# A third raw weight buffer and a token-by-token end of each second product, in a fused retention, routing and MLP kernel

## The chip, the cores and the metric

The kernel runs on one core of a Trainium2 chip. The metric is the device time of one execution in microseconds (us). TensorE (PE, with its weight loads as PEld) does the matrix products, VectorE (DVE), ScalarE (ACT) and GpSimd (POOL) the elementwise work, and SyncE (SP) issues most of the transfers. Each engine runs its own instructions strictly in their order and waits on semaphores for the others.

## The reference

```
x = retention(q, k, v)              # 8 x 8 heads, 576 positions, to 4608 tokens x 512
logits = x @ w_gate                 # 8 experts, each takes exactly 576 tokens, greedily by logit
for e in range(8):
    out[mask_e] = relu(x[mask_e] @ w1[e]) @ w2[e]        # 512 -> 1024 -> 512
h = relu(out @ w_in)                # 512 -> 2048
return (h * h) @ w_out              # 2048 -> 512
```

All data are float32 and all large products have float32 accuracy: each operand is split into a rounded high part and the rest (the low part), and a product is made of three: high weights by high data, low weights by high data, high weights by low data (PAIRS).

## The kernel before, in words

**Attention** (0 to about 165 us of the profiled execution) makes x in transposed tiles X, and converts the second MLP's weights into a DRAM tensor wd beside it. The table `rt` of 510 columns, which the router needs, comes in one transfer among the first loads (line 108), and `Router.start` makes constants from its later columns after the fourth token tile. Then the router places the tokens of the first expert, and x goes to DRAM token by token (xd).

**The main part** (218 to 1514 us) goes expert by expert. `moe(k)` works on the 576 tokens of expert k in two parts of 288. Each part has eight steps f: a first product into a PSUM tile `mm` (line 802, 12 matmuls of 288 columns), the relu and split of its result into the tile `h` (ACT L807, DVE L808), and the second product of the step two before (LAG = 2) into four accumulators `acc` (L785, 12 matmuls). After the last second product of a part the accumulators are copied to YH by ACT (L791) and their rest to YL by DVE (L792). There are four `acc` buffers, so the first second product of part 1 waits until YL has been taken of part 0. That place is called the part border below.

After each expert one or two blocks `mlp(j)` of 384 tokens follow, twelve in all (j = 0 to 11: one after experts 0, 2, 4, 6, two after 1, 3, 5, 7). A block has 16 steps: first product (L865, 12 matmuls of 384 columns), then ACT L871 (relu), DVE L873 (square), ACT L875 (high part of h), DVE L842 (low part of h, called `low`), and the second product two steps late (L849, 9 matmuls: three token tiles by three pairs). At the end of a block two second products are left, those of f = 14 and f = 15. They run one after the other, and after f = 15 ACT copies each token tile's accumulator to `ot` (L853), which POOL scatters to the output (L828).

**The weight stream.** Weights come in chunks of 128 x 1024 float32, 16 per expert and 7 per block (nine of the 16 MLP chunks stay on chip, tile `big`). `pump()` is called once per step. It splits one chunk, if one has been fetched and the weight tiles have room: ACT writes the high parts of w1 and w2 (L628, two instructions), POOL the low part of w1 (L629), DVE the low part of w2 (L630). Then it fetches one chunk into a buffer `raw` (SP, L639), if fewer than two are fetched and not split. There are two `raw` buffers, so the transfer of chunk i waits until ACT, POOL and DVE are done with chunk i - 2.

```
if i < st["fetched"] and i < st["used"] + 3 and not fetch_only:
    raw = raws.pop(i)
...
    nc.gpsimd.tensor_sub(w1[:, 1], raw[:, :512], w1[:, 0].bitcast(F32))
    nc.vector.tensor_sub(w2[:, 1], raw[:, 512:], w2[:, 0].bitcast(F32))
...
if i < len(stream) and i < st["split"] + 2:
```

**The router** for expert k + 1 runs in small pieces (`slot`) between the products of expert k and the following blocks: comparisons on DVE (L398, L427, L432), small matmuls on PE into `rps` (L421, L431, L480). It is done for experts 0 to 7 before expert 6's products, so experts 6 and 7 run without it. Tokens of the next expert are gathered from xd (POOL) and turned on PE (L716).

The order of every engine's instructions is that of the program; there is no scheduler.

Of the kernel before, what the change touches and what calls it, by code (L numbers as in the profile page):

```python
# [6 lines left out]
F32 = mybir.dt.float32  # L7
R = mybir.dt.float32r
# [61 lines left out]
def attention(tc, a, X, idn, rt, filler):  # L70

    nc = tc.nc
    L = rt.L
    with ExitStack() as c:
# [30 lines left out]
        wg = cn.tile([128, 4, 32], F32, name="wg")  # L105
        nc.vector.memset(wg, 0.0)
        nc.sync.dma_start(wg[:, :, :NE], a["wg"])
        nc.sync.dma_start(rt.f, a["rt"])
        load(3, 0, 2)
        load(2, 2, 3)  # L110
        load(4, 0, 2)
# [111 lines left out]
        for t in range(NT):  # L223
            if t + 2 < NT:
                turn_k(t + 2)
            if t + 1 < NT:
                weigh(t + 1)
                scores(t + 1)
            if t + 5 < NT:
                load(t + 5, 0, 2)  # L230
            if t + 3 < NT:
                load(t + 3, 2, 3)
            if t + 2 < 9:
                decay(t + 2)
            before(t)
            if t >= 4 and t % 2 == 0:
                next(todo, None)
            values(t)
            if t % 9 != 8:
                state(t)  # L240
            if t == NT - 2:
                ready = rt.prep(0, 32)
            if t >= NT - 2:
                next(ready)
            if t == 3:
                rt.start()
            next(filler, None)
        last = [gate(32, 35), gate(35, 36, "sp")]
        for g in last:
# [7 lines left out]
def route_tables():  # L257
    i = np.arange(128)
    tri = (i[:, None] < i[None, :]).astype(np.float32)
    u = np.zeros((128, 72), np.float32)  # L260
    j = np.arange(72)
    u[:72] = j[:, None] < j[None, :]
    thr = np.zeros((4, 16), np.float32)
    off = 0
    for r, step in enumerate(STEPS):
        thr[r] = np.arange(16) * step - off
        off += step
    sel = np.zeros((128, 4, 8), np.float32)
    for tl in range(4):
        sel[tl * 8:tl * 8 + 8, tl] = np.eye(8)  # L270
    f = np.concatenate([np.tile(thr.reshape(1, 64), (128, 1)),
                        np.tile(8.0 - np.arange(8), (128, 1)),
                        np.tile(128.0 * np.arange(36), (128, 1)),
                        i[:, None].astype(np.float32),
                        np.zeros((128, 8)),
                        np.tile(np.arange(8.0), (128, 1)),
                        np.tile(i, (128, 1)),
                        tri, u,
                        i[:, None] // 16 == np.arange(8),
                        i[:, None] % 16 == np.arange(16),  # L280
                        np.where(i < 8, CAP, BIG)[:, None],
                        sel.reshape(128, 32),
                        ], axis=1)
    return np.ascontiguousarray(f, np.float32)


# [6 lines left out]
class Router:  # L293
# [6 lines left out]
    def __init__(self, tc, pool):  # L300
        self.nc, self.ps = tc.nc, None
        t = pool.tile
        self.L = t([128, NT, 8], F32, name="L")
        f = self.f = t([128, 510], F32, name="rt")
        self.thr = f[:, 0:64].rearrange("p (r j) -> p r j", r=4)
        self.w8 = f[:, 64:72]
        self.t128 = f[:, 72:108]
        self.pcol = f[:, 108:109]
        self.e8 = f[:, 117:125]
        self.m8, self.m16 = f[:, 453:461], f[:, 461:477]  # L310
        self.c8 = f[:, 477:478]
        self.io = t([128, 128, 12], FH, name="io")
        self.b = t([128, 128 + 72], FH, name="rtb")
        self.tri, self.u = self.b[:, 0:128], self.b[:, 128:200]
        self.OH = [t([128, 128, 12], FH, name=f"OH{i}") for i in range(2)]
        self.sel = self.OH[0].rearrange("p s t -> p (s t)")[:, :512].rearrange("p (t m) -> p t m", t=4)
        self.ones = t([128, 128], FH, name="ones")
        self.U = t([128, NT], F32, name="U")
        self.AS = t([128, NT], F32, name="AS")
        self.C = t([128, 8], F32, name="C")  # L320
        self.idx = t([128, NT], I32, name="idx")
        self.es = t([1, NE], I32, name="es")
        self.A = t([128, NT + 12, 8], FH, name="A")
        self.V = t([128, NT, 8], F32, name="V")
        self.m = t([128, NT], F32, name="m")
        self.vm = t([128, NT], F32, name="vm")
        self.vu = t([128, NT], F32, name="vu")
        self.ki = t([128, 4, NT], I32, name="ki")
        self.kf = t([128, 2, NT], F32, name="kf")
        self.k2 = t([128, NT], F32, name="k2")  # L330
        self.B = t([128, 2], F32, name="B")
        self.G = t([128, NT + 4, 16], FH, name="G")
        self.c4 = t([128, 64], FH, name="c4")
        self.S8 = t([128, 16], FH, name="S8")
        self.dg = t([128, 8, 8], F32, name="dg")
        self.cc = t([128, 8], F32, name="cc")
        self.cx = t([128, 16, 8], FH, name="cx")
        self.cf = t([128, 16, 8], F32, name="cf")
        self.jm = t([128, 16], F32, name="jm")
        self.jk = t([128, 16], F32, name="jk")  # L340
        self.GT = t([128, 2, NT], F32, name="GT")
        self.NEW = t([128, 2, NT, 8], FH, name="NEW")
        self.wn = t([128, 16], FH, name="wn")
        self.nn = t([128, 48], F32, name="nn")
        self.DT = t([128, 2, NT], FH, name="DT")
        self.tot = t([72, 128], FH, name="tot")
        self.sl = t([128, 4, NT], F32, name="sl")
        self.si = t([128, 3, NT], I32, name="si")
        self.sb = t([128, 2, NT], FH, name="sb")
        self.h5 = t([128, NT, 5], FH, name="h5")  # L350
        self.HC = t([128, NT, 10], FH, name="HC")
        self.ids = t([128, 10], F32, name="ids")

    def start(self):
        v, f = self.nc.vector, self.f
        for x, c in ((self.sel, 0.0), (self.ones, 1.0), (self.U, 1.0), (self.AS, 0.0), (self.C, float(CAP)),
                     (self.A, 0.0), (self.G, 0.0)):
            v.memset(x, c)
        v.tensor_copy(self.io, f[:, 125:253].unsqueeze(2).to_broadcast([128, 128, 12]))
        v.tensor_copy(self.b, f[:, 253:453])  # L360
        v.tensor_copy(self.sel[:, :, 0:8], f[:, 478:510].rearrange("p (t e) -> p t e", t=4))

    def p(self):
        return self.ps.tile([128, 128], F32, name="rps")
# [220 lines left out]
def body(tc, a, out):  # L585
    nc = tc.nc
    with ExitStack() as ctx:
# [8 lines left out]
        rt = Router(tc, gp)  # L596
# [23 lines left out]
        def pump(fetch_only=False):  # L620

            i = st["split"]
            if i < st["fetched"] and i < st["used"] + 3 and not fetch_only:
                raw = raws.pop(i)
                w1 = wk.tile([128, 2, 512], R, name="w1", bufs=3)
                w2 = wk.tile([128, 2, 512], R, name="w2", bufs=5)
                for w, c in ((w1, raw[:, :512]), (w2, raw[:, 512:])):
                    nc.scalar.activation(w[:, 0], c, AF.Copy)  # L628
                nc.gpsimd.tensor_sub(w1[:, 1], raw[:, :512], w1[:, 0].bitcast(F32))  # L629
                nc.vector.tensor_sub(w2[:, 1], raw[:, 512:], w2[:, 0].bitcast(F32))  # L630
                chunks[i] = (w1, w2)
                st["split"] += 1
            i = st["fetched"]
            if i < len(stream) and i < st["split"] + 2:
                kind, k, f = stream[i]
                if kind == "e" and k not in ev:
                    return
                raw = raws[i] = wk.tile([128, 1024], F32, name="raw", bufs=2)
                nc.sync.dma_start(raw, wd[f] if kind == "m"  # L639
                                  else a["we"][bass.ds(ev[k], 1), f].rearrange("o p c -> (o p) c"))  # L640
                st["fetched"] += 1
# [135 lines left out]
        def moe(k):  # L777
# [16 lines left out]
            for part in range(2):  # L794
                turned(5 * k + (5 if part else 3))
                for f in range(8):
# [6 lines left out]
                                             X[xi][:, g, 288 * part:288 * part + 288],  # L803
                                             start=(g == 0 and i == 0), stop=(g == 3 and i == 2))
                    slot(True)
                    h = wk.tile([128, 2, 384], R, name="h", bufs=4)
                    nc.scalar.activation(h[:, 0, :288], p[:, :288], AF.Relu)  # L807
                    nc.vector.scalar_tensor_tensor(h[:, 1, :288], p[:, :288], 0.0, h[:, 0, :288].bitcast(F32),  # L808
                                                   op0=OP.max, op1=OP.subtract)
# [24 lines left out]
        def mlp(j):  # L834
# [6 lines left out]
                    s, h = lows.pop()  # L841
                    nc.vector.tensor_sub(h[:, 1], s, h[:, 0].bitcast(F32))  # L842

            def mm2(f, w2, h):
                if f == 0:
                    acc.extend(ps.tile([128, 512], F32, name="acc", bufs=4) for _ in range(3))
                for t in range(3):
                    for i, (wi, xi) in enumerate(PAIRS):
                        nc.tensor.matmul(acc[t], h[:, xi, t * 128:(t + 1) * 128], w2[:, wi],  # L849
                                         start=(f == 0 and i == 0), stop=(f == 15 and i == 2))  # L850
# [5 lines left out]
            for f in range(16):  # L856
# [14 lines left out]
                nc.scalar.activation(r, p[:, :384], AF.Relu)  # L871
                s = r
                nc.vector.tensor_mul(s, p[:, :384], r)  # L873
                h = wk.tile([128, 2, 384], R, name="h", bufs=4)
                nc.scalar.activation(h[:, 0], s, AF.Copy)  # L875
                lows.append((s, h))
                q.append((f, w2, h))
# [3 lines left out]
                low()  # L881
                if f >= LAG:
                    slot()
            while q:
                mm2(*q.pop(0))

        turner, keeper, parter = turn_back(), stay(), part()
        while 0 not in listed:
# [38 lines left out]
```

## Time and profile before

| | us |
|---|---|
| median of 3 runs | 1531.27 (1529.21 to 1531.87) |
| the profiled execution | 1525.86 |
| its span, first to last instruction | 1524.1 |
| PE busy in it | 1462.2 (96%) |
| DVE busy | 963.5 (63%) |
| ACT busy | 675.0 (44%) |
| POOL busy | 468.5 (31%) |

The span is what the trace shows; the execution's own time has 1.8 us around it. A busy PE is not a PE at its peak, since matmuls overlap: what counts below is the time in which PE waits, and for whom. The mean granted TensorE clock of the execution was 0.992.

### The profile page before, as it was taken

The numbers are of one execution on the slowest core, as the hardware profiler recorded it, in microseconds if no ns is written. First come the engines' busy times: TensorE is split into PE (matmuls) and PEld (weight loads), VectorE is DVE, ScalarE is ACT, GpSimd is POOL, SyncE is SP. The second block draws the span as 40 slices with busy tenths as digits, with TensorE's granted clock in tenths as the row PEclk, the third lists the DMA queues.
The fourth block names the chain that finished last, engine by engine and source line by source line (L and its number), as shares of the span: only waits on it lengthen the run. The fifth ranks groups of instructions, "written<-read, shape, count | busy, mean of one in ns | idle before, by whom it ended". The sixth has DMA issues, their size and how long they took to land.

```text
span 1524.1 us, 27399 instructions
## 1 busy us (share of the span) xinstructions
PE 1462.2 (96%) x10599; PEld 1324.4 (87%) x10599; DVE 963.5 (63%) x1965; ACT 675.0 (44%) x1349; POOL 468.5 (31%) x410
## 2 busy tenths in 40 slices
PE   7998879999999999999999999999999999999997
PEld 6777768888988898889988899899888999999896
DVE  5999768766765657557765667567646455454341
ACT  6766644444433434334433344344334344444332
POOL 4454134544312224124213143233122431242110
PEclk9999979999999999999999999999999999999999
DMA  9999567224511224225313143234112351252110
GB/s 337 347 365 352 197 203 257 97 70 133 158 56 72 87 93 154 70 97 157 107 56 96 58 148 127 68 123 161 56 61 89 123 174 64 64 180 95 57 49 21
DMA packets 64210, 201.14 MB, mean 132 GB/s; under 512 B 8400, under 2 KB 8656, under 8 KB 64080
## 3 DMA queue, kind: packets, MB, share of 16 engines
q1 hardware_dynamic: 58128, 179.99, 35.2%
q0 software_dynamic: 5952, 19.40, 3.6%
q8 instruction: 83, 1.36, 0.4%
q14 instruction: 47, 0.39, 0.1%
HBM read 172.10 MB, written 27.26 MB: 131 GB/s over the span
## 4 chain that ended last, share of the span: by engine, by line
PE 73%; DVE 11%; DMA 6%; issue 5%; ACT 4%; POOL 0%; SPq 0%; ACTq 0%; DVEq 0%; POOLq 0%
PE mm L865 24%; PE acc L849 23%; PE acc L785 9%; PE mm L802 8%; DMA raw<-we 4%; DVE w L630 3%; PE px L205 2%; ACT w L628 1%; PE sc L165 1%; PE mm L716 1%; PE rps L508 1%; DVE cb L569 1%; DVE G L398 1%; DVE A L169 1%; DMA raw<-wd 1%
## 5 line engine op out<-in xcount | busy, mean ns | idle before, releaser
L629 POOL TENSOR_TENSOR w<-raw,w 128x512 fp32r<-128x512 f32 x212 | 278.0, 1311 | 825.8 <-ACT w L628 729.0
L630 DVE TENSOR_TENSOR w<-raw,w 128x512 fp32r<-128x512 f32 x212 | 265.4, 1252 | 228.7 <-ACT w L628 224.4
L628 ACT ACTIVATE w<-raw 128x512 fp32r<-128x512 f32 x424 | 243.3, 621 | 205.7 <-DMA raw<-we 163.0
L849 PE MATMUL acc<-big,h 128*128 128x512 f32 x972 | 246.0, 397 | 0.0
L785 PE MATMUL acc<-h,w 128*128 128x288 f32 x1536 | 224.4, 296 | 12.0 <-DVE YL L792 9.7
L785 PEld LDWEIGHTS acc<-h,w 128*128 128x128 f32 x1536 | 208.4, 188 | 14.6 <-DVE YL L792 11.6
L849 PEld LDWEIGHTS acc<-big,h 128*128 128x128 f32 x972 | 180.1, 188 | 35.4 <-DVE h L842 0.3
L871 ACT ACTIVATE r<-mm 128x384 f32<-128x384 f32 x192 | 93.9, 489 | 237.7 <-PE mm L865 217.2
L875 ACT ACTIVATE h<-r 128x384 fp32r<-128x384 f32 x192 | 100.9, 525 | 216.8 <-DVE r L873 216.8
L849 PE MATMUL acc<-w,h 128*128 128x512 f32 x756 | 190.9, 396 | 2.9 <-DVE h L842 2.9
L873 DVE TENSOR_TENSOR r<-mm,r 128x384 f32<-128x384 f32 x192 | 105.9, 551 | 125.5 <-ACT r L871 125.3
L865 PE MATMUL mm<-YH,big 128*128 128x384 f32 x864 | 173.4, 342 | 0.0
L849 PEld LDWEIGHTS acc<-w,h 128*128 128x128 f32 x756 | 139.3, 188 | 29.6 <-DVE h L842 3.7
L802 PE MATMUL mm<-XH,w 128*128 128x288 f32 x1024 | 161.0, 300 | 0.8 <-ACT XH L724 0.7
L865 PEld LDWEIGHTS mm<-YH,big 128*128 128x128 f32 x864 | 152.1, 188 | 7.7 <-ACT YH L791 0.9
L842 DVE TENSOR_TENSOR h<-r,h 128x384 fp32r<-128x384 f32 x192 | 110.9, 577 | 65.7 <-ACT h L875 65.7
L802 PEld LDWEIGHTS mm<-XH,w 128*128 128x128 f32 x1024 | 143.8, 190 | 2.0 <-ACT XH L724 1.1
L865 PE MATMUL mm<-YH,w 128*128 128x384 f32 x672 | 133.3, 339 | 0.0
L865 PEld LDWEIGHTS mm<-YH,w 128*128 128x128 f32 x672 | 117.6, 188 | 4.3
L865 PE MATMUL mm<-YL,big 128*128 128x384 f32 x432 | 93.4, 338 | 0.0
L802 PE MATMUL mm<-XL,w 128*128 128x288 f32 x512 | 89.0, 295 | 0.0
L865 PEld LDWEIGHTS mm<-YL,big 128*128 128x128 f32 x432 | 77.3, 188 | 0.3 <-DVE YL L792 0.2
(171 smaller groups left out, 1713.5 us busy)
## 6 DMA issues: line engine op xcount, KB each, us to landing
raw<-we SPq DMA_DIRECT2D x128, 512.0 KB, 3.6
raw<-wd SPq DMA_DIRECT2D x84, 512.0 KB, 3.2
qk<-att SPq DMA_DIRECT2D x36, 512.0 KB, 7.0
craw<-wm SPq DMA_DIRECT2D x32, 512.0 KB, 6.7
v<-att SPq DMA_DIRECT2D x36, 256.0 KB, 5.4
wd<-cb SPq DMA_DIRECT2D x32, 256.0 KB, 5.4
xd<-YH SPq DMA_DIRECT2D x18, 256.0 KB, 3.5
xd<-YL SPq DMA_DIRECT2D x18, 256.0 KB, 3.6
```

The lines of the kernel that those rows point to most:

```text
L205: nc.tensor.matmul(px[o:o + 64, g, :], V[t][:, g, lo:lo + 64], D[t]["A"][i][:, g, :], start=(ph == 0), stop=True)
L628: nc.scalar.activation(w[:, 0], c, AF.Copy)
L629: nc.gpsimd.tensor_sub(w1[:, 1], raw[:, :512], w1[:, 0].bitcast(F32))
L630: nc.vector.tensor_sub(w2[:, 1], raw[:, 512:], w2[:, 0].bitcast(F32))
L785: nc.tensor.matmul(acc[part][d][:, :288], w2[:, wi, d * 128:(d + 1) * 128], h[:, xi, :288], start=(f == 0 and i == 0), stop=(f == 7 and i ...
L802: nc.tensor.matmul(p[:, :288], w1[:, wi, g * 128:(g + 1) * 128], X[xi][:, g, 288 * part:288 * part + 288], start=(g == 0 and i == 0), stop ...
L842: nc.vector.tensor_sub(h[:, 1], s, h[:, 0].bitcast(F32))
L849: nc.tensor.matmul(acc[t], h[:, xi, t * 128:(t + 1) * 128], w2[:, wi], start=(f == 0 and i == 0), stop=(f == 15 and i == 2))
L865: nc.tensor.matmul(p[:, :384], w1[:, wi, g * 128:(g + 1) * 128], Y[xi][:, g, o:o + 384], start=(g == 0 and i == 0), stop=(g == 3 and i == 2))
L871: nc.scalar.activation(r, p[:, :384], AF.Relu)
L873: nc.vector.tensor_mul(s, p[:, :384], r)
L875: nc.scalar.activation(h[:, 0], s, AF.Copy)
```

## The change

A third `raw` buffer is made and `pump` fetches up to three chunks that are not split. Its room comes from two places: `h` has three buffers in place of four, and the router's table is taken in two transfers, of which the larger (`rf`, 360 columns) lies in the attention's pool and is given up with it. In `mlp` the last two second products are taken token tile by token tile: f = 14 and 15 for tile 0, then for tile 1, then for tile 2.

```
-        nc.sync.dma_start(rt.f, a["rt"])
+        nc.sync.dma_start(rt.f, a["rt"][:, :150])
+        rf = cn.tile([128, 360], F32, name="rf")
+        nc.sync.dma_start(rf, a["rt"][:, 150:])
...
-                rt.start()
+                rt.start(rf)
...
-            if i < len(stream) and i < st["split"] + 2:
+            if i < len(stream) and i < st["split"] + 3:
...
-                raw = raws[i] = wk.tile([128, 1024], F32, name="raw", bufs=2)
+                raw = raws[i] = wk.tile([128, 1024], F32, name="raw", bufs=3)
...
-                    h = wk.tile([128, 2, 384], R, name="h", bufs=4)
+                    h = wk.tile([128, 2, 384], R, name="h", bufs=3)
...
-            def mm2(f, w2, h):
+            def mm2(f, w2, h, tiles=range(3)):
...
-                for t in range(3):
+                for t in tiles:
...
-                h = wk.tile([128, 2, 384], R, name="h", bufs=4)
+                h = wk.tile([128, 2, 384], R, name="h", bufs=3)
...
-            while q:
-                mm2(*q.pop(0))
+            for t in range(3):
+                for x in q:
+                    mm2(*x, tiles=(t,))
```

The orders of DVE, ACT and POOL do not change: every instruction stands where it stood. Two orders change. On PE, at the end of each block, here the fourth (j = 3, after expert 2), whose last two second products read a streamed weight tile `w` (f = 14) and a kept one `big` (f = 15). Before:

```order
L421 MATMUL rps<-A,G 128x64
L849 MATMUL acc<-w_7786,h 128x512 x9
L849 MATMUL acc<-big,h 128x512 x9
L802 MATMUL mm<-XH,w_7862 128x288 x8
L802 MATMUL mm<-XL,w_7862 128x288 x4
L716 MATMUL mm<-idn,xg 128x128 x4
```

and in the changed kernel (its line numbers are 3 higher here):

```order
L424 MATMUL rps<-A,G 128x64
L852 MATMUL acc<-w_7790,h 128x512 x3
L852 MATMUL acc<-big,h 128x512 x3
L852 MATMUL acc<-w_7790,h 128x512 x3
L852 MATMUL acc<-big,h 128x512 x3
L852 MATMUL acc<-w_7790,h 128x512 x3
L852 MATMUL acc<-big,h 128x512 x3
L805 MATMUL mm<-XH,w_7866 128x288 x8
L805 MATMUL mm<-XL,w_7866 128x288 x4
L719 MATMUL mm<-idn,xg 128x128 x4
```

The first matmul that reads the last h (f = 15) moves from the tenth place of these 18 to the fourth, and the last matmul of tile 0 from the twelfth to the sixth, that of tile 1 from the fifteenth to the twelfth.

On SP, each fetch stands one fetch earlier against everything else in the queue. Here the end of expert 1 and the two blocks behind it, where `raw<-we` is an expert's chunk, `raw<-wd` an MLP chunk, and the load of `es` reads the router's choice of expert. Before:

```order
L639 ISA
L639 DMA raw<-we 128x1024
L639 DMA raw<-wd 128x1024 x9
L697 TENSOR_LOAD es
L697 ISA x2
L639 DMA raw<-wd 128x1024 x5
L639 ISA
L639 DMA raw<-we 128x1024
```

and in the changed kernel:

```order
L642 ISA
L642 DMA raw<-we 128x1024
L642 DMA raw<-wd 128x1024 x10
L700 TENSOR_LOAD es
L700 ISA x2
L642 DMA raw<-wd 128x1024 x4
```

Ten MLP chunks stand ahead of the load of `es` where nine stood, and no fetch has moved behind a wait that it did not stand behind.

## Rows read from the trace of the kernel before

**Rows 1.** The page: its head and PE's row, busy us and share.

```profile
span 1524.1 us, 27399 instructions
...
PE 1462.2 (96%) x10599; PEld 1324.4 (87%) x10599; DVE 963.5 (63%) x1965; ACT 675.0 (44%) x1349; POOL 468.5 (31%) x410
```

**Rows 2.** PE's waits: who waited for whom, us in total, times, longest us.

```profile
PE acc L785 <- DVE YL L792: 9.7, 8, 1.7
...
PE rps L431 <- DVE cx L427: 2.9, 6, 1.1
...
PE acc L785 <- DVE h L808: 2.3, 2, 1.5
```

**Rows 3.** Waits of all engines, same columns.

```profile
DVE w L630 <- ACT w L628: 224.4, 156, 3.2
...
ACT w L628 <- DMA raw<-we: 163.0, 88, 6.0
...
ACT w L628 <- DMA raw<-wd: 39.6, 22, 3.1
```

**Rows 4.** Chain that ended last, expert 6 from 1223 us: start, us, what.

```profile
1223.47 3.56 DMA raw<-we
...
1228.30 1.38 DVE w L630
...
1229.78 3.32 DMA raw<-we
...
1238.36 1.59 PE mm L802 x12
```

**Rows 5.** Timeline, expert 6's part border: start, us, engine line [idle before, releaser].

```profile
1233.19 1.15 ACT L628 ACTIVATE w<-raw 128x512 fp32r<-128x512 f32 x2 [1.84 <-DMA raw<-we]
...
1234.37 1.36 DVE L630 TENSOR_TENSOR w<-raw,w 128x512 fp32r<-128x512 f32 x1 [1.56 <-ACT w L628]
...
1236.03 1.53 DVE L792 TENSOR_TENSOR YL<-acc,YH 128x288 fp32r<-128x288 f32 x4
...
1236.52 1.84 PE L785 MATMUL acc<-h,w 128*128 128x288 f32 x12 [1.30 <-DVE YL L792]
```

**Rows 6.** Timeline, expert 0's part border.

```profile
252.46 1.46 DVE L630 TENSOR_TENSOR w<-raw,w 128x512 fp32r<-128x512 f32 x1 [0.24 <-ACT w L628]
...
258.00 1.85 PE L785 MATMUL acc<-h,w 128*128 128x288 f32 x12 [1.72 <-DVE YL L792]
```

**Rows 7.** Timeline, expert 1's part border, whose wait is the shortest.

```profile
391.71 1.06 PE L785 MATMUL acc<-h,w 128*128 128x288 f32 x6 [0.58 <-DVE YL L792]
```

**Rows 8.** Durations of two DVE groups: count, ns least/median/most, first and last start.

```profile
L630 DVE TENSOR_TENSOR w<-raw,w x212: 672/1365/2487, 205.4 to 1481.1; 128x512 fp32r<-128x512 f32 x106
...
L427 DVE TENSOR_TENSOR cx<-cc,rt x48: 291/292/1367, 230.6 to 1090.9; 128x128 f16<-128x128 f32 x48
```

**Rows 9.** Timeline, end of block j = 3: second product f = 14, then h of f = 15.

```profile
679.18 2.31 PE L849 MATMUL acc<-w,h 128*128 128x512 f32 x9
...
679.86 0.52 ACT L875 ACTIVATE h<-r 128x384 fp32r<-128x384 f32 x1 [1.75 <-DVE r L873]
680.41 0.56 DVE L842 TENSOR_TENSOR h<-r,h 128x384 fp32r<-128x384 f32 x1 [0.59 <-ACT h L875]
...
681.33 2.26 PE L849 MATMUL acc<-big,h 128*128 128x512 f32 x9
```

**Rows 10.** Timeline, end of block j = 0, the same instructions.

```profile
355.79 0.52 ACT L875 ACTIVATE h<-r 128x384 fp32r<-128x384 f32 x1 [2.09 <-DVE r L873]
356.35 0.56 DVE L842 TENSOR_TENSOR h<-r,h 128x384 fp32r<-128x384 f32 x1 [0.59 <-ACT h L875]
...
356.48 2.37 PE L849 MATMUL acc<-big,h 128*128 128x512 f32 x9
```

**Rows 11.** Timeline, end of block j = 2, the same instructions.

```profile
550.47 2.30 PE L849 MATMUL acc<-w,h 128*128 128x512 f32 x9
550.48 0.53 ACT L875 ACTIVATE h<-r 128x384 fp32r<-128x384 f32 x1 [1.51 <-DVE r L873]
```

**Rows 12.** Timeline, the end of the last block and the tail of the kernel.

```profile
1508.90 0.53 ACT L875 ACTIVATE h<-r 128x384 fp32r<-128x384 f32 x1 [0.62 <-DVE r L873]
...
1509.63 2.23 PE L849 MATMUL acc<-w,h 128*128 128x512 f32 x9
...
1512.59 2.00 ACT L853 ACTIVATE ot<-acc 128x512 f32<-128x512 f32 x3 [3.16 <-PE acc L849]
1513.46 0.99 POOL L828 DMA_INDIRECT out<-ot,idx  x1 [31.48 <-ACT ot L853]
...
1516.03 0.97 POOL L828 DMA_INDIRECT out<-ot,idx  x1 [0.22 <-issue]
```

**Rows 13.** Timeline, the first microseconds: the router's table, the next load, PE.

```profile
7.64 0.34 SPq L108 DMA_DIRECT2D rt<-rt  x1
...
8.02 0.43 SPq L85 DMA_DIRECT2D qk<-att  x1
...
15.56 0.66 PE L143 MATMUL pr<-idn,qk 128*128 128x128 f32 x4
```

More of the change, by code (lines that the diff above doesn't have):

```diff
@@ L283, in route_tables @@
                         ], axis=1)
+    f = np.concatenate([f[:, :125], f[:, 453:478], f[:, 125:453], f[:, 478:]], axis=1)
     return np.ascontiguousarray(f, np.float32)
@@ L303, in __init__ @@
         self.L = t([128, NT, 8], F32, name="L")
-        f = self.f = t([128, 510], F32, name="rt")
+        f = self.f = t([128, 150], F32, name="rt")
         self.thr = f[:, 0:64].rearrange("p (r j) -> p r j", r=4)
@@ L309, in __init__ @@
         self.e8 = f[:, 117:125]
-        self.m8, self.m16 = f[:, 453:461], f[:, 461:477]
-        self.c8 = f[:, 477:478]
+        self.m8, self.m16 = f[:, 125:133], f[:, 133:149]
+        self.c8 = f[:, 149:150]
         self.io = t([128, 128, 12], FH, name="io")
@@ L352, in __init__, with start @@
         self.ids = t([128, 10], F32, name="ids")
-    def start(self):
-        v, f = self.nc.vector, self.f
+    def start(self, f):
+        v = self.nc.vector
         for x, c in ((self.sel, 0.0), (self.ones, 1.0), (self.U, 1.0), (self.AS, 0.0), (self.C, float(CAP)),
@@ L358, in start @@
             v.memset(x, c)
-        v.tensor_copy(self.io, f[:, 125:253].unsqueeze(2).to_broadcast([128, 128, 12]))
-        v.tensor_copy(self.b, f[:, 253:453])
-        v.tensor_copy(self.sel[:, :, 0:8], f[:, 478:510].rearrange("p (t e) -> p t e", t=4))
+        v.tensor_copy(self.io, f[:, 0:128].unsqueeze(2).to_broadcast([128, 128, 12]))
+        v.tensor_copy(self.b, f[:, 128:328])
+        v.tensor_copy(self.sel[:, :, 0:8], f[:, 328:360].rearrange("p (t e) -> p t e", t=4))
     def p(self):
```

## Prediction

> **What bounds the kernel now.** I read the page first. PE is busy for 1462.2 of 1524.1 us [rows 1], so no change of transfers can give more than the 62 us between them, and only where PE itself waits. The waits of PE come next. The largest is at the part border: the first second product of part 1 waits for YL, eight times, once per expert, 9.7 us in all [rows 2]. Behind it, and also within the experts' stages, stand waits for DVE's router work (L431 for cx, 2.9 us) and for h (2.3 us) [rows 2]. No row has PE waiting for a weight tile.
>
> Weights still matter, one step removed. In the waits of all engines ACT's split waits 163.0 us for expert chunks and 39.6 us for MLP chunks, and DVE's part of the split waits 224.4 us for ACT [rows 3]. Both engines are in order, so whatever stands behind the split waits too. The chain of waits of expert 6, which runs without a router, shows what sets that pace: transfer 3.56 us, ACT, DVE 1.38 us, and the next transfer into the same buffer, 6.31 us from 1223.47 to 1229.78 [rows 4]. With two buffers that is 3.16 us a chunk. PE needs 1.59 us for the 12 matmuls of a first product [rows 4] and as much for those of a second, 3.18 us a step. The loop and PE are tied, and the loop never gets ahead.
>
> At the part border this lateness reaches PE. In expert 6 ACT's split starts at 1233.19 after 1.84 us of waiting for the chunk, DVE's part after 1.56 us for ACT, YL comes at 1236.03, and PE has waited 1.30 us when it starts at 1236.52 [rows 5].
>
> **The third raw buffer.** Nothing is added on ACT, POOL or DVE: their orders are the same, word for word. What changes is when a chunk lands. With three buffers the loop of 6.31 us [rows 4] carries three chunks, 2.1 us each, against 3.2 us of PE per step; a chunk then lies ready about 3 us before its split, and ACT splits it as soon as it comes to it. In expert 6 the split at 1233.19 would start 1.84 us earlier, DVE's part at least 1.56 us earlier, and 1.56 is more than the 1.30 that PE waited: the wait goes.
>
> What the eight borders give has two ends. The lower: DVE can move forward by at least its own wait before L630, and that is least in expert 0, 0.24 us against a PE wait of 1.72 [rows 6]; in the other seven I grant no more than the shortest PE wait of all, 0.58 in expert 1 [rows 7]. That is 0.24 + 7 x 0.58 = 4.3 us. The upper is all of 9.7. I take 8.0: seven of the eight look like expert 6, and in expert 0 much of DVE's time at the border is router work that stays.
>
> The two other waits of rows 2, 2.9 + 2.3 = 5.2 us, lie between 0 and 5.2. They end with DVE work that stands behind a late L630 but is itself long; I take 1.5, nearer to nothing, since there DVE is mostly busy and not waiting.
>
> In the MLP blocks a chunk is needed only every second or third step, and ACT's wait there is a fraction of the 39.6 us, none of it in front of PE: nothing.
>
> **The token-by-token end.** Here is a cost. Before, the first matmul on h of f = 15 had all nine of f = 14 in front of it; now three. Take block j = 3 [rows 9]. Nine matmuls last from 679.18 to 681.33, 0.24 us each. After three PE is at 679.90. The high part of h is done at 679.86 + 0.52 = 680.38. From the end of that instruction to PE's start I take 0.17 us, as in block 0 where the high part ends at 356.31 and PE starts at 356.48 [rows 10]. So PE waits until 680.55, 0.65 us; after two matmuls it is at 681.03, and the low part (680.97 + 0.17 = 681.14) costs 0.11 more. 0.76 us, and block 6 shows the same pattern: 1.5 us together. In block 0 PE had already waited for this h, and the six matmuls of f = 14 that filled the time until 356.48 now come after it: PE does two matmuls on the high part, waits to 357.08 for the low part, and has 13 left where it had 9 - the end moves from 356.48 + 9 x 0.24 = 358.64 to 357.08 + 13 x 0.24 = 360.20, 1.5 us. In blocks 2 and 5 the high part is ready at 551.01 + 0.17 for a PE at 550.47 + 0.71 [rows 11], just in time, and the low part costs 0.1 each. In the other seven it is early; in the last one the high part is done at 1509.43 and wanted at 1510.3 [rows 12]. The sum is 1.5 + 1.5 + 0.2 = 3.2 us. Bounds: 2 us, if the earlier chunks also relieve ACT and DVE in block 0; 5.6, if blocks 1, 4 and 7 fall to the state of block 3 (3 x 0.8 more).
>
> **The tail.** In the last block tile 0 is finished six matmuls earlier, tile 1 three. Today ACT copies three tiles from 1512.59, 0.67 us each, and POOL scatters them from 1513.46, one each 1.29 us, the last at 1516.03 [rows 12]. With tile 0 earlier by 6 x 0.23 = 1.4 us the first two scatters are over by 1514.5, and the third waits only for its own copy: last matmul as before, copy until 1514.65, scatter at 1514.85. That is 1.2 us off the end. It cannot be more, since the third tile ends as before, and nothing if POOL's queue has another delay.
>
> **Edits at no cost.** Three h buffers: h of step f takes the buffer of f - 3, whose second product stands ahead of the first product of f on PE, and ACT waits for that one anyway. The second transfer of the table costs SP another 0.34 us behind 7.64 and moves the load at 8.02 [rows 13]; PE first reads that load at 15.56, 7.5 us later. If the cover failed it would be about 0.4 us, once.
>
> **A rule that speaks against it.** DVE's L630 takes 0.672 us at best and 1.365 in the median, and cx (L427) 0.292 in the median and 1.367 at worst [rows 8]: something holds DVE for about the length of another engine's instruction. The Trainium skill, page "SBUF — State Buffer", section "SBUF: two separate sides", says that DVE with two SBUF inputs and GpSimd lock one shared pair of ports, whole instruction by whole instruction. By that rule a POOL split that runs earlier leaves L630 and hits router work in its stead; the trace agrees that such hits exist (cx 1.367), and no run here shows how many there would be. It is the slower rival below, and is not in the sum.
>
> **The sum.** -8.0 (borders) - 1.5 (other waits) + 3.2 (block ends) - 1.2 (tail) = -7.5 us. The profiled execution, 1525.86 with its span of 1524.1, would be 1518.4 with a span of 1516.6. It lies 5.4 us under the median of the three timed runs, so I take the difference to the median: 1531.27 - 7.5 = 1523.8 us. With all gains at their best and the block ends at 2: 9.7 + 5.2 + 1.2 - 2 = 14.1 less, 1517.2. With all at their worst: 4.3 less and 5.6 more, 1532.6.
>
> **The rivals.** About 0.2% (3.1 us) is what a measurement of this kernel can tell from no change.
> - DVE, not the chunk, holds the border. For it: the routers run in experts 0 to 5, and in expert 0 the wait for the chunk was only 0.24 of 1.72 us [rows 6]. Against it: expert 6 without a router waits 1.30 [rows 5]. Gains then are 3.0 at the borders and 1.2 at the tail, the cost 3.2: 1531.27 - 1.0 = 1530.3 us. Chance 0.17.
> - The third buffer does not make chunks early, because the transfers themselves are slower with one more under way. For it: a transfer in the loop takes 3.3 to 3.6 us already [rows 4]. Against it: three chunks in 6.3 us leave a third of the time over. Only the block ends and the tail remain: +3.2 - 1.2 = 1533.3 us. Chance 0.08.
> - Slower: POOL's earlier splits hit DVE's router work in experts 0 to 5. One hit is 1.367 - 0.292 = 1.1 us [rows 8]. It costs only where PE waits for that piece. Ten more such hits, among the 96 chunks of these six experts, eat the 7.5 us and 3.1 beyond; with ten to twelve it would be about 1535 us. Against it: L630 itself gets shorter by up to 0.69 us where the hit leaves it. Chance 0.07.
>
> **How the numbers follow.** The forecast has 0.68. Nearly all of it is faster by over 0.2% (below 1528.2); with a little of the first rival faster is 0.68, the same 0.24 (most of the first two rivals), slower 0.08. The range of the forecast alone is 1518 to 1529; to hold 8 in 10 it goes on to the first rival, 1518 to 1530.5, and leaves out the other two and what lies below.
>
> **What would show it.** Right: ACT's wait for raw falls from 202.6 us to under 40; PE's wait for YL from 9.7 to under 3; a new wait of PE L852 for ACT h or DVE h at the ends of blocks 0, 3 and 6, 2 to 4 us in all; the last scatter 1.2 us nearer to the last matmul. Wrong: YL's wait still near 9 us with chunks early (first rival), ACT's wait for raw still over 100 us (second), cx or L398 longer on average and PE's waits for `rps` grown by 8 us or more (third). What would make the number wrong with the mechanism right is the share of the 5.2 us of router waits that goes, and block ends that are later than here.

## The result and the profile after

The changed kernel takes 1511.61 us (median of four runs, 1509.73 to 1512.18), the kernel before 1530.4 beside it (1529.21 to 1531.87). The ratio is 0.9883 with a 95% interval of 0.9858 to 0.9908: faster by 1.2%, 18.8 us. The prediction was 1523.8 us, 7.5 us faster, with 1518.0 as the lower end of its range. The direction was right, the size less than half.

The profiled execution after took 1512.18 us, 13.7 us less than that of before. The page's head, PE's row and DVE's part of the split (these answer to [rows 1] and [rows 8]):

```profile
span 1510.4 us, 27450 instructions
...
PE 1461.7 (97%) x10599; PEld 1325.1 (88%) x10599; DVE 933.6 (62%) x1965; ACT 688.6 (46%) x1349; POOL 468.6 (31%) x410
...
L633 DVE TENSOR_TENSOR w<-raw,w 128x512 fp32r<-128x512 f32 x212 | 226.9, 1070 | 193.5 <-ACT w L631 192.5
```

PE's work is the same to 0.5 us; what went is its idle time. DVE is busy 30 us less although it runs the same instructions in the same order.

PE's waits after, in the columns of [rows 2]:

```profile
PE acc L852 <- DVE h L845: 2.9, 2, 1.5
...
PE acc L852 <- ACT h L878: 1.8, 3, 1.1
...
PE rps L434 <- DVE cx L430: 0.7, 2, 0.5
```

The largest row of before, PE for YL (9.7 us), is gone from the list altogether, as is the wait for DVE's h in the experts (2.3). The wait for cx fell from 2.9 to 0.7. The three waits for ACT's h at the ends of blocks, 1.8 us, are new: they are the price of the new order. DVE's h above them stood there before with the same 2.9, and is not of the new order.

The waits of the other engines, in the columns of [rows 3]:

```profile
DVE w L633 <- ACT w L631: 192.5, 140, 1.6
...
ACT w L631 <- PE acc L788: 62.1, 93, 1.4
...
ACT w L631 <- DMA raw<-we: 15.8, 17, 2.6
```

ACT's wait for an expert chunk fell from 163.0 to 15.8 us. In its place stands a wait for PE's second products, 62.1 us: the chunk now lies ready so early that the split waits for a weight tile to come free. DVE still waits 192.5 us for ACT, but by at most 1.6 us at a time where it was 3.2, and no row of PE waiting for YL is left.

Expert 6's chain of waits shows it at a glance, beside [rows 4]. It was a loop of transfer and split; now PE is all of it, row after row:

```profile
1220.85 1.58 PE acc L788 x12
1222.43 1.60 PE mm L805 x12
1224.03 1.58 PE acc L788 x12
1225.61 1.60 PE mm L805 x12
1227.21 1.58 PE acc L788 x12
```

At its part border the timeline, beside [rows 5], reads:

```profile
1222.46 0.63 ACT L631 ACTIVATE w<-raw 128x512 fp32r<-128x512 f32 x1 [0.65 <-PE acc L788]
1223.13 0.69 DVE L633 TENSOR_TENSOR w<-raw,w 128x512 fp32r<-128x512 f32 x1 [1.34 <-ACT w L631]
...
1224.90 1.64 DVE L795 TENSOR_TENSOR YL<-acc,YH 128x288 fp32r<-128x288 f32 x4
...
1227.04 1.74 PE L788 MATMUL acc<-h,w 128*128 128x288 f32 x12
```

DVE's part is over at 1223.82, YL begins at 1224.90, and its first piece is done well before PE asks for it at 1227.04. Before, YL began at 1236.03 for a PE that had wanted it at 1235.2.

The end of block 0, beside [rows 10], and then the windows around it (columns: window, its length, busy us of PE, PEld, DVE, ACT and POOL with counts, the granted share of TensorE's clock, DMA share, GB/s):

```profile
355.83 1.39 PE L852 MATMUL acc<-big,h 128*128 128x512 f32 x3 [1.12 <-ACT h L878]
...
357.02 1.48 PE L852 MATMUL acc<-w,h 128*128 128x512 f32 x3
358.30 1.48 PE L852 MATMUL acc<-big,h 128*128 128x512 f32 x3
359.58 0.94 PE L852 MATMUL acc<-w,h 128*128 128x512 f32 x3
```

```profile
349.00:356.00 7.00, 4.43 (x25) 3.00 (x25) 4.73 (x10) 2.95 (x6) 1.30 (x2) 1.00 0.12 38
356.00:360.00 4.00, 4.00 (x11) 2.99 (x12) 1.06 (x4) 0.78 (x2) 1.01 (x1) 0.57 0.25 99
```

Three matmuls take 1.28 us from 357.02 to 358.30, where [rows 9] has 0.24 each. The granted clock is 0.57 in that window, mostly the lower of TensorE's levels (1.2 GHz), after a stretch in which PE was busy for 4.43 of 7 us. In the profile before the same stretch had 5.55 us of PE and the clock stayed at 1.00.

The tail, beside [rows 12]:

```profile
1497.11 0.85 PE L852 MATMUL acc<-w,h 128*128 128x512 f32 x3
...
1499.57 0.99 POOL L831 DMA_INDIRECT out<-ot,idx  x1 [29.94 <-ACT ot L856]
...
1502.35 0.97 POOL L831 DMA_INDIRECT out<-ot,idx  x1 [0.33 <-ACT ot L856]
```

From the first matmul of f = 14 to the last scatter there are now 5.24 us, where there were 1516.03 - 1509.63 = 6.40. The difference is the 1.2 us forecast.

### The profile page after: what moved, and what is told of

Its sections match the earlier page's. It is cut to its first block, busy times and chain, and to the rows that moved or that the text cites. A ratio compares the mean times of both kernels' runs of the same rounds, so it can differ in the third digit from the quotient of the medians.

```text
span 1510.4 us, 27450 instructions
## 1 busy us (share of the span) xinstructions
PE 1461.7 (97%) x10599; PEld 1325.1 (88%) x10599; DVE 933.6 (62%) x1965; ACT 688.6 (46%) x1349; POOL 468.6 (31%) x410
## 3 DMA queue, kind: packets, MB, share of 16 engines
q8 instruction: 83, 1.36, 0.4%
## 4 chain that ended last, share of the span: by engine, by line
PE 84%; DVE 7%; issue 4%; ACT 3%; DMA 1%; POOL 0%; SPq 0%; POOLq 0%; DVEq 0%; ACTq 0%
PE mm L868 25%; PE acc L852 24%; PE acc L788 13%; PE mm L805 13%; PE px L207 2%; PE sc L167 1%; PE mm L719 1%; PE rps L511 1%; DVE cb L572 1%; DVE G L401 1%; DVE A L171 1%; DVE w L633 1%; PE px L199 1%; ACT cb L564 1%; PE pr L145 1%
## 5 line engine op out<-in xcount | busy, mean ns | idle before, releaser
L633 DVE TENSOR_TENSOR w<-raw,w 128x512 fp32r<-128x512 f32 x212 | 226.9, 1070 | 193.5 <-ACT w L631 192.5
L631 ACT ACTIVATE w<-raw 128x512 fp32r<-128x512 f32 x424 | 253.1, 623 | 78.3 <-PE acc L788 62.1
L852 PE MATMUL acc<-big,h 128*128 128x512 f32 x972 | 251.2, 399 | 1.8 <-ACT h L878 1.8
L852 PE MATMUL acc<-w,h 128*128 128x512 f32 x756 | 196.0, 398 | 2.9 <-DVE h L845 2.9
L810 ACT ACTIVATE h<-mm 128x288 fp32r<-128x288 f32 x128 | 52.5, 410 | 103.2 <-PE mm L805 97.8
```

## The experiments

The theory: with two buffers a chunk is late, ACT and DVE pass the lateness on, and PE pays at the part border and in the router's pieces; the third buffer ends that. The rivals: the new order at the block ends carries the gain; or what makes room for the buffer does; or the lead in program order.

Where stages are compared below, a stage runs from the first matmul of its first product to that of the next stage, read from the timeline of each profile. In us:

| stage | before | before again | after | third buffer alone | held, two | held, three | last block only |
|---|---|---|---|---|---|---|---|
| expert 0 | 62.36 | 63.60 | 59.54 | 59.87 | 67.04 | 60.80 | 59.88 |
| expert 1 | 54.26 | 54.00 | 53.17 | 53.18 | 54.40 | 53.17 | 53.18 |
| expert 2 | 56.98 | 56.34 | 52.77 | 52.78 | 57.72 | 52.78 | 52.78 |
| expert 4 | 55.65 | 56.18 | 52.82 | 52.82 | 55.09 | 52.83 | 52.82 |
| expert 6 | 52.47 | 52.27 | 50.72 | 50.72 | 59.60 | 51.77 | 50.72 |
| expert 7 | 52.22 | 51.76 | 50.72 | 50.72 | 59.04 | 50.72 | 50.72 |
| block 0 | 78.34 | 78.32 | 82.24 | 79.08 | 78.31 | 79.51 | 79.15 |
| block 3 | 71.75 | 71.74 | 72.31 | 71.60 | 71.75 | 71.60 | 71.61 |
| block 11 and tail | 77.35 | 77.35 | 75.93 | 77.10 | 77.35 | 77.10 | 75.94 |

**The kernel before, once more.**

> The kernel before, unchanged, profiled once more. Its first profiled execution took 1525.86 us while its timed runs have a median of 1530.4. If the difference is of the chunk loop (two buffers tied to PE's pace, so that any slower transfer costs PE time), this profile shows longer waits of PE for YL and router work than the first (9.7 and 5.2 us), by some 4 us together, at a like clock. If it is of TensorE's clock, the waits are like those of the first and the trace has more stretches at the lower clock, some 1.5 us of loss each. Ratio to itself 1.000.

Median 1528.2 us, ratio to itself 0.9998 (0.9986 to 1.001). The profile has a span of 1524.9 us, PE waits 10.4 us for YL, and the clock is not lowered between 224 us and the tail, as in the first. So neither of the two answers came out: both profiled executions lie below the middle of a wide field. Beside it the kernel before ran 29 times, from 1523.89 to 1532.32 us, 8.4 us apart. The third buffer alone ran four times, within 3.0 us, too few to compare the two widths: a repeat of the changed kernel, below, spread over 4.9 us in five runs, nine of the kernel before beside it over 5.9. The stages show the width better: with two buffers expert 2 took 56.34 to 58.31 us in six profiles, with three buffers 52.77 to 52.80 in eight.

**The third buffer alone.** The changed kernel with this edit taken back:

```
-            for t in range(3):
-                for x in q:
-                    mm2(*x, tiles=(t,))
+            while q:
+                mm2(*q.pop(0))
```

> The change without the token-by-token end of the blocks: three raw buffers, three chunks ahead, three h buffers, the table in two transfers. If late chunks were the cause, all of the gain and the cost of the block ends besides: about 18.8 + 4 - 1 = 20 to 23 us below before, and no wait of PE for YL. If the gain came from the new order of the last second products, near 0.

1508.65 us, ratio 0.9876 (0.9858 to 0.9895): 19.3 us faster, slightly under the span expected, and no row of PE waiting for YL. The gain is here.

**The block ends alone.** The kernel before, with the `tiles` argument and the three lines above put in.

> The kernel before with the token-by-token end of the blocks alone; two raw buffers, four h buffers, one table. Theory of late chunks: slower by the block ends less the tail, +3.2 - 1.2 = 2 us, up to 5 us where PE's wait at the end of block 0 also lowers the clock. Rival (the ends carry the gain): faster by over 5 us.

1528.4 us, ratio 1.0006 (0.9995 to 1.0016): the same. The 2 us expected are not excluded by that interval. Its stages cost about what was worked out: block 0 79.65 for 78.3, blocks 3 and 6 0.7 each, and block 11 76.19 for 77.35.

**What makes room, alone.** The changed kernel with

```
-            if i < len(stream) and i < st["split"] + 3:
+            if i < len(stream) and i < st["split"] + 2:
...
-                raw = raws[i] = wk.tile([128, 1024], F32, name="raw", bufs=3)
+                raw = raws[i] = wk.tile([128, 1024], F32, name="raw", bufs=2)
```

and the block ends as before.

> Only what makes room: three h buffers and the table in two transfers; two raw buffers, two chunks ahead, block ends as before. Theory: within 1 us of before. Rival (the smaller first transfer or the h buffers matter): more than 2 us either way.

1527.34 us, ratio 0.9994 (0.9984 to 1.0004): nothing. Since the third buffer alone has the same room and gained 19.3 us, the gain comes with the buffer and the longer lead.

**Three buffers, lead of two.** The changed kernel with the first of those two lines alone.

> The changed kernel with three raw buffers, but pump again fetches only up to two chunks that are not split. SP runs through its queue on its own and waits only for a free buffer, so by the theory of late chunks the third buffer does the work and the lead in program order hardly counts: within 3 us of the changed kernel (ratio 0.986 to 0.990). Rival (the lead counts): most of the gain gone, ratio over 0.995.

1512.85 us, ratio 0.9898 (0.9881 to 0.9914), and experts 1 to 7 in the same times to 0.03 us. SP waits 1025.5 us in all for DVE's part of the split, which frees the buffers, and 95.6 us for the router's choice of expert (1083.7 and 34.8 with a lead of three), and the experts do not feel the difference: the lead in program order is not needed.

**Chunks fetched twice,** in experts 6 and 7, with two buffers and with three:

```
-                nc.sync.dma_start(raw, wd[f] if kind == "m"
+                for _ in range(2 if kind == "e" and k > 5 else 1):
+                    nc.sync.dma_start(raw, wd[f] if kind == "m"
```

> The kernel before (two buffers) with every chunk of experts 6 and 7 fetched twice into its buffer. If the loop of transfer and split sets these experts' pace, 1.5 to 3.4 us more per loop are 0.75 to 1.7 us a chunk over a loop that has no slack: with some 30 chunks 22 to 50 us slower than before. If PE or DVE sets it and the transfer has slack, under 5 us.

> Three buffers, three chunks ahead, block ends as before, and every chunk of experts 6 and 7 fetched twice. The loop of 6.3 + 1.5 to 3.4 us carries three chunks, 2.6 to 3.2 us each, against 3.18 us of PE per step: within 5 us of the same kernel with single fetches (ratio 0.9876). Rival (the transfers have no room for more under way): over 15 us slower than that.

Two buffers: 1580.86 us, ratio 1.0334 (1.031 to 1.0357), 52 us slower, just over the upper end. Three: 1538.83 us, ratio 1.007 (1.0053 to 1.0087), some 30 us over the same kernel with single fetches: the rival's number. The chain of waits with three buffers shows why:

```profile
1207.50 4.21 DMA raw<-we
...
1211.72 3.67 DMA raw<-we
```

The second transfer into a buffer was issued only when the first had landed, and SP, in order, stood there with the other buffers' fetches behind it. So the chunks come about one landing apart, as the starts of ACT's splits show:

```profile
1210.54 1.15 ACT L631 ACTIVATE w<-raw 128x512 fp32r<-128x512 f32 x2 [3.47 <-DMA raw<-we]
...
1215.48 1.15 ACT L631 ACTIVATE w<-raw 128x512 fp32r<-128x512 f32 x2 [3.48 <-DMA raw<-we]
```

That is 4.94 us a chunk, where PE needs 3.18. The experiment lengthened SP's queue and not only the loop, so the pair decides nothing on the third buffer.

**Buffers held longer,** the same question without that fault. The chunk is stored from its buffer by a transfer that ACT issues behind its part of the split (the stored data are not used):

```
                     nc.scalar.activation(w[:, 0], c, AF.Copy)
+                if stream[i][0] == "e" and stream[i][1] > 5:
+                    nc.scalar.dma_start(spare[i % 32], raw[:, :512])
```

> The kernel before (two buffers); in experts 6 and 7 each chunk is also stored to a spare DRAM tensor from its raw buffer, issued by ACT right behind its two instructions, so that no queue waits longer but the buffer is held for one more transfer. With about 3.5 us for the store in place of DVE's 1.4 the loop is 3.4 + 1.2 + 3.5 = 8.1 us, 4.05 a chunk with two buffers against 3.18 of PE: some 14 chunks x 0.9 = 12 us more in each of the two experts, 52.2 to about 64 us, 24 us in all. Rival (the buffer loop does not set the pace): under 2 us per expert.

> The same stores with three buffers, three chunks ahead, block ends as before. The loop of 8.1 us carries three chunks, 2.7 us each, under PE's 3.18: experts 6 and 7 stay at 50.7 to 51.5 us. Rival (the third buffer's gain is not room in the loop): each expert longer by about as much as with two buffers.

Two buffers: 1540.44 us, ratio 1.008 (1.0056 to 1.0104), 12.5 us slower where 24 were expected. Three: 1508.65 us, ratio 0.9879 (0.9861 to 0.9898), what it took without the stores. Experts 6 and 7 took 59.60 and 59.04 us with two buffers, 7.3 more than in the second profile of before, and 51.77 and 50.72 with three. The chain with two buffers shows the longer loop:

```profile
1223.75 3.46 DMA raw<-we
...
1227.36 3.40 DMA spare<-raw
...
1230.89 3.42 DMA raw<-we
```

From fetch to fetch this is 7.14 us; the next two loops of the same chain take 7.77 and 7.18, so the mean is 7.36, 3.68 a chunk. The store starts with ACT's part and not behind it, so the loop is shorter than the 8.1 I had expected, and (3.68 - 3.18) x 16 = 8.0 us over PE's pace is near the 8.9 by which expert 6 is over its 50.72. In each of the two experts the granted clock also fell once for 3.4 us (from 1245.5 and 1375.2), and how much of the 7.3 that is was not separated. Expert 0's 67.04 in this profile is not of the stores, which run in experts 6 and 7 alone: 6.8 us at the lower clock, from 259.1, fell into it. Over three buffers 7.36 us is 2.5 a chunk, below PE's 3.18, and there the stores cost 1.05 us in expert 6 and nothing in expert 7. This settles it: the two-buffer loop has no slack, the three-buffer loop has.

**The new order in the last block alone:**

```
+            if j < 11:
+                while q:
+                    mm2(*q.pop(0))
             for t in range(3):
                 for x in q:
                     mm2(*x, tiles=(t,))
```

> The changed kernel with the token-by-token end in the last block (j = 11) alone. Theory: blocks 0, 3 and 6 lose their new waits, so 71.60 us in blocks 3 and 6 and 77.5 to 79.1 in block 0 (as without the new order), while block 11 keeps 75.9: 1.2 us better than the three buffers alone, ratio about 0.986 to 0.987. Rival (the order helps elsewhere too, for instance by earlier scatters): slower than the three buffers alone.

1506.69 us, ratio 0.9859 (0.9842 to 0.9875). Block 0 is at 79.15, blocks 3 and 6 at 71.61, block 11 keeps 75.94. Once more, beside the changed kernel on one chip:

> The changed kernel once more, on the same chip as the next: ratio to before 0.988; block 0 at 82 us with the clock lowered at its end, or about 80.4 without.

> The changed kernel with the new order in the last block alone, once more beside the changed kernel: lower than it by the ends of blocks 0, 3 and 6, 1.3 + 0.7 + 0.7 = 2.7 us, and some 1.6 more where the clock falls at the end of block 0.

The changed kernel 1510.28 us, ratio 0.989 (0.9871 to 0.9909), block 0 at 81.00; this one 1506.5, ratio 0.9865 (0.9847 to 0.9884). The two intervals overlap, but the stages are plain: blocks 0, 3 and 6 differ by 1.6, 0.7 and 0.7 us, and nothing else of the main part by over 0.25. Its ratio is the lowest here; that of the third buffer alone (0.9858 to 0.9895) overlaps it.

## Why the prediction was wrong in its size

The forecast fell 11.3 us short of the 18.8. Of these 6.2 lie between the two profiles, 13.7 us apart where the sum had 7.5: the two other waits (3.0), what a wait costs beyond its length (2.9) and the borders (1.7), less 1.3 of the first stage and 0.1 of the blocks and the tail. The other 5.1 lie in the base.

**The bound and the mechanism: right.** The first step, that two buffers tie the chunk loop to PE's pace and that PE pays for it behind ACT and DVE, is shown by the third buffer alone, and by the held buffers with two and with three. The split's wait for raw fell from 202.6 to 15.8 us (its row for MLP chunks is gone), under the 40 that were named as the sign.

**The borders, -8.0: too small.** All 9.7 us went, in expert 0 too. I had left 1.7 us there to the router's work on DVE.

**The two other waits, -1.5: the term of the sum that failed most.** They are 5.2 us [rows 2], and I took 1.5, "since there DVE is mostly busy and not waiting". Measured, 4.5 went: 2.9 to 0.7 and 2.3 to nothing. (Another router wait, PE for G in L421, L424 after, rose from 0.3 to 1.6.) DVE's busy time was not as fixed as I took it. The median of DVE's part of the split went from 1365 ns to 1058, in the list of durations by tile:

```profile
L633 DVE TENSOR_TENSOR w<-raw,w x212: 673/1058/2489, 207.8 to 1468.8; 128x512 fp32r<-128x512 f32 x106
```

In all, 226.9 us where the page of before has 265.4 for the same group. It goes with the third buffer: with that alone the group takes 227.5, with what makes room alone 265.3. The border of expert 6 shows one such instruction, beside POOL's part of the same split, first before (to be read with [rows 5]), then after:

```profile
1233.89 1.29 POOL L629 TENSOR_TENSOR w<-raw,w 128x512 fp32r<-128x512 f32 x1 [2.00 <-ACT w L628]
```

```profile
1221.89 1.28 POOL L632 TENSOR_TENSOR w<-raw,w 128x512 fp32r<-128x512 f32 x1 [1.89 <-ACT w L631]
```

Before, DVE starts at 1234.37 while POOL is at work until 1235.18, and takes 1.36 us. After, ACT's second instruction waits for a weight tile, DVE starts at 1223.13 when POOL's part is all but over (1223.17), and takes 0.69. How much of the 4.5 us is due to the shorter instructions and how much to the earlier chunk no run here separates.

The slower rival's hits came as well. Here is cx in the groups by line, busy us and mean ns, before and after:

```profile
L427 DVE TENSOR_TENSOR cx<-cc,rt 128x128 f16<-128x128 f32 x48 | 19.4, 403 | 1.7
```

```profile
L430 DVE TENSOR_TENSOR cx<-cc,rt 128x128 f16<-128x128 f32 x48 | 23.7, 494 | 1.7
```

The median hides it (293 ns for 292). But what cx lost, 4.3 us, is far less than the 38.5 that DVE's part of the split gained, and PE's waits for the router's `rps`, which that rival had growing by 8 us or more, went from 14.4 to 13.0 us in all. The Trainium skill's rule of the shared ports ("SBUF — State Buffer", section "SBUF: two separate sides") agrees with instructions that take 0.69 us alone and twice that beside POOL. The shift that the prediction drew from it took place both ways, and in sum it went in DVE's favour.

**What a wait costs: not in the sum.** I had counted each us of waiting as one us of time. The eight experts took 17.1 us less between the two profiles (443.2 to 426.1, all eight stages summed), while the waits in the rows that I had priced fell by 9.7 + 2.2 + 2.3 = 14.2, and PE's idle time in those stages, read from the traces, by 13.0 (15.7 to 2.7). In expert 6 a wait of 1.30 us was 1.75 us of its stage. Of that the border's own distance shows 1.45: start to start of the two matmuls around it, less the usual one. Why a wait costs more than its idle time no run here shows.

**The block ends, +3.2, and the tail, -1.2: right in sum by luck, the parts not.** Blocks and tail together changed by +2.1 us between the two profiles, for +2.0 forecast: block 0 cost 2.4 us more than forecast, and the blocks without a new wait (1, 2, 4, 5 and 7 to 10) came out 1.5 us shorter together, which I had not forecast. With what makes room alone, on two buffers, the same blocks are 1.3 us shorter. Blocks 3 and 6 cost 0.56 and 0.55 (0.7 against three buffers with the old order; 0.76 forecast), the tail 1.2 as forecast. Block 0 cost 3.9 and not 1.5: with the clock at 1.00 the new order alone costs it 1.3 (79.65 for 78.3), and the other 2.6 come with lowered clock. Twice 3.4 us at the lower level (1.2 GHz), from 305.1 and from 356.3, fell into this block. The first has nothing to do with the order, as the third buffer alone has it too (304.9, block 0 at 79.08), and what makes room alone (308.2, 79.05). The second falls behind the new wait. That it is the wait that lowers the clock is argued from the windows above and not shown: in the repeat of the changed kernel the clock fell there too (353.9, block 0 at 81.0), and with a lead of two (354.5, for 6.8 us, block 0 at 82.32); with the old order it did not at the end of block 0 in any profile. But with the new order on two buffers it stayed up as well, with the same two waits (1.44 and 1.12 us) and PE busy for 4.44 of the 7 us from 349 to 356.

**Edits at no cost: right.** What makes room alone is within noise. The first stage to 218 us was 1.3 us longer in the profile after; it varied from 215.3 to 220.0 over all profiles, with no clear relation to the edits.

**The base: the largest single part.** I made the sum against a profiled execution of 1525.86 us, said that it lay 5.4 under the median, and carried the difference over. That assumed that the changed kernel's profile would lie as low; it lay 0.6 us above its median. The profile pair differs by 13.7 us, the medians by 18.8. With two buffers the eight experts took 441.0 to 446.6 us together in the four profiles without doubled fetches or stores, with three 426.1 to 426.7 in six. That the landing of the transfers makes this width is argued and not shown. A gain that differs from execution to execution could not be read from one fast execution. Part of the 18.8 may be chance: in the repeat the medians lay 17.7 us apart (1527.93 and 1510.28).

## What to carry to other kernels

Here a transfer loop that only just kept PE's pace did not show as PE waiting for data. It showed as in-order engines that waited for it and passed the lateness to unrelated work behind; price all of that work, and the spread of the runs, not only the one wait that is plainly behind the late chunk. Divide the time of the loop (landing, all readers of the buffer, next issue) by the number of buffers and ask for a margin over the consumer's step. Finishing tiles early at the end of a block cost time here wherever PE then had to wait for the last h (blocks 0, 3 and 6). It paid in the last block, where that h was ready and the copies and scatters behind it ended the kernel.

## What the runs showed of the hardware that was not expected

- TensorE's clock fell for 3.4 us after short waits alone: granted 0.57 in 356 to 360 us, after 4.43 us of work in the 7 before, with no wait over 1.46 us. Three matmuls of 512 columns then took 1.28 us start to start, for 3 x 0.24 at 1.00. With the new order on two buffers the same waits left the clock at 1.00, so the waits alone do not decide it.
- A second transfer into the same buffer held SP until the first had landed: 4.21 us and then 3.67, one after the other, with the next chunk's fetch behind.
- DVE's part of the split took 0.69 us where POOL's part was all but over, and 1.36 beside it. Chunks that landed earlier moved many of these instructions off POOL's: the median fell from 1365 to 1058 ns, 38.5 us in all.
- With two buffers expert 2's stage varied by 2 us from one profile to the next; with three, experts 1 to 7 repeat to 0.03 us (the profiles with stores or doubled fetches aside).
